# Shifts of integer score copies on one vector engine: two buffers an instruction, in place of a share on GpSimd

## Chip, cores and metric

One core of a Trainium2 chip. The metric is device time in microseconds (us). The kernel before has a median of 401.99 us over 4 runs (400.75 to 402.68). A measurement of this kernel can tell a difference of about 0.3% from none.

## What is computed

Two independent attention layers over 2048 tokens of width 448 with 16 heads of 28; the outputs are put side by side.

```python
def A(x, wq, wk, wv, wo):            # all heads share one k and one v
    q = (x @ wq) split in 16 heads;  k = x @ wk;  v = x @ wv
    p = softmax(q @ k.T * 28 ** -0.5)
    return concat_heads(p @ v) @ wo
def B(x, wqkv, wo):                  # each token sees itself and 7 tokens, 2 apart, before it
    q, k, v = split of x @ wqkv, 16 heads each
    return concat_heads(softmax over 8 positions (q . k) @ v) @ wo
out = concatenate([A(A_x, ...), B(B_x, ...)], axis=-1)
```

## The kernel before, in words

A is the bulk: 16 heads x 2048 queries x 2048 keys. Its scores are made in blocks of 128 keys by 512 queries, transposed, so that keys lie on partitions. There are 16 groups (4 stretches of 512 queries by 4 sets of 4 heads), and each has 64 blocks (16 key tiles by 4 heads): 1024 blocks. One matmul makes a block; up to four of them run beside each other on TensorE, one a strip of 32 rows (the QK step, `do_qk`, L1479). Each block then needs an exponential, and there are two ways:

- On ScalarE, an Exp from PSUM over two or three blocks at once (`act_choose`, L1227). Its five PSUM banks form two rings, of 3 and of 2 banks, which take turns. The result is in P.
- On VectorE, the code's D jobs (`dread`). A drain (L1526, name `dr`) turns the scores of a block, from one PSUM bank, into 16-bit integers that, read as bf16, are a coarse power of two. The result is the first of four variants in a buffer Z. Two more instructions, SBUF to SBUF, make the other variants: the first shift (L1534, `s1`) adds 32 to variant 0 and gives variant 1 (512 elements a partition); the second (L1541, `s2`) adds 64 to variants 0 and 1 and gives 2 and 3 (1024 elements). There are NZ = 6 such buffers. The four variants are multiplied by four differently weighted copies of v (WJ), which averages the coarseness out.

The PV step (`do_pv`, L1589) multiplies P or Z blocks by v, again up to four beside each other, and gathers a group in one PSUM bank. A closed group goes through `chain`: VectorE copies the bank to a buffer PVs (L988), SP sends the row of denominators to `den` by a DMA, VectorE takes reciprocals (L1004), SP sends them to DRAM and back, spread over partitions, to `bc`, and GpSimd or VectorE multiplies (L1034, `mul`). `outproj` (L662) multiplies by wo, VectorE or ScalarE moves the result to an output buffer (L1090, L1088), and SP or ScalarE issues the DMA to the output. B has 16 score blocks (L1320), each with an Exp on ScalarE (L1343) and a minimum with a mask (L1340), and its own PV step (L1287). Projections of both layers (L662) are "fills": work for TensorE between the QK steps.

The order on every engine is settled when the program is built. A planner in the kernel keeps a clock for each engine and lets the engine that is furthest behind pick its next step (`pe_choose`, `act_choose`, `spec_choose`), from costs and due times that are constants at the top of the file. `SCHED` resets some of these constants at given planned times. A few matter here. A drain's shifts wait in one list for VectorE or GpSimd; GpSimd takes a first shift only when VectorE's backlog is at least `GPB` = 1500 planned ns, and the second shift of a buffer stays on the engine that made the first. `put` with `port=True` keeps such VectorE and GpSimd steps from overlapping in the plan. A fill that is overdue may run over the planned start of the next QK step by up to `FTOL` ns. `DWAIT` says how long a QK step may be held for a bank for a D job. `dummy` (L1672, L1674) puts matmuls on zeros or weights whose result isn't used where TensorE's planned activity of the last 3.4 us is under `HAMLOW`. Each engine runs its list in order; a step waits on semaphores for what it reads and overwrites.

At the start (`plan_start`), the first 512 rows of x come in by two DMAs, from SP and from ScalarE's queue, each for all 128 partitions and two of the four rows that a partition holds. TensorE transposes them (L682); the other rows come by transposing DMAs on SP. GpSimd's queue makes constants, issues the DMAs of wB (B's weights, 1.2 MB), and then fills wB's unused part, woA, woB and `one` by memsets.

Of the kernel before, what the change touches and what calls it, by code (L numbers as in the profile page):

```python
# [6 lines left out]
ALU = mybir.AluOpType  # L7
AX = mybir.AxisListType
BF16 = mybir.dt.bfloat16
# [4 lines left out]
D = 448  # L14
# [31 lines left out]
def bk0(b, half):  # L46
# [3 lines left out]
    if b == 0 and half == 0:  # L50
# [6 lines left out]
AHEAD = 2  # L57
BT0 = 87
BDT = 38
DRATE = 0.3  # L60
# [3 lines left out]
TOL = 40.0  # L64
DWAIT = 100.0
FTOL = 250.0
FSAFE = 300.0
# [4 lines left out]
GP_S2 = 1010.0  # L72
GPB = 1500.0
GP_TT16 = 1010.0
# [8 lines left out]
HAMW = 3413.0  # L83
HAMLOW = 0.5
HAMTILE = 0.55
LATE = 1000.0
RINGD = 0.25
RINGB = 1200.0
PRESS = 2
PV3 = 8  # L90
JOBO = 0.0
JOBL = 1.0
XL0 = 4300.0
FILLN = 120.0
FILL0 = 8.0
FRATE = 0.036
FQUIET = 70

SCHED = ((0, {'HAMLOW': 0.5, 'HAMTILE': 0.55, 'FILLN': 120.0, 'FILL0': 8.0, 'PV3': 8, 'RINGB': 1200.0, 'PRESS': 2, 'DWAIT': 100.0, 'FTOL': 250.0, 'TOL': 40.0, 'JOBO': 0.0, 'LATE': 1000.0, 'FSAFE': 300.0}),
         (300, {'HAMLOW': 0.6, 'FTOL': 400.0, 'TOL': 20.0}),  # L100
         (330, {'FTOL': 250.0, 'TOL': 40.0, 'LATE': -5.0}),
         (355, {'HAMLOW': 0.5, 'FILL0': 4.0, 'RINGB': 1800.0, 'PRESS': 1, 'DWAIT': 300.0, 'LATE': 1000.0}),
         (375, {'HAMLOW': 0.8, 'FILL0': 8.0, 'RINGB': 1200.0, 'PRESS': 2, 'DWAIT': 200.0}))
VB0 = 27.0
WO0 = 70
# [48 lines left out]
class Spec:  # L154


    def __init__(self, engs, reads, writes, make, prio, dur, gate, name, hold, port):
        self.engs = engs
        self.reads = reads
        self.writes = writes  # L160
        self.make = make
        self.prio = prio
        self.dur = dur
        self.gate = gate
        self.name = name
        self.hold = hold
        self.port = port


# [33 lines left out]
class _Gen:  # L203
# [233 lines left out]
    def alloc(self, es):  # L437
# [28 lines left out]
        self.mask = sb([128, 2, 512], BF16, "mask")  # L466
        self.NPV = 4
        self.PVs = sb([128, self.NPV, 512], FP32, "PVs")
# [9 lines left out]
        self.oTnB = sb([128, 4, 4, 512], BF16, "oTnB")  # L478
        self.NO = 3
        self.ob = sb([128, self.NO, D], BF16, "ob")  # L480
        self.nr = sb([128, 2, 512], BF16, "nr")
# [19 lines left out]
    def plan_start(self):  # L501
        g = self
# [22 lines left out]

        def xA(q, b0, b1, lands):
            self.dma_op(q, g.xn[:, b0:b1, :], g.A_x[0, 0:512, :].rearrange("(p b) c -> p b c", b=4)[:, b0:b1, :],
                        writes=[res("xn")] if b0 == 0 else (), appends=[res("xn")] if b0 else (), lands=lands, name="x")
        xA("sp", 0, 2, XL0)
        xA("act", 2, 4, XL0)  # L530
        wA("act", g.wq, g.A_wq, D, "wq", 4500.0)
# [3 lines left out]
        for c in range(1, 4):  # L535
            for kt in range(4):
                self.dma_op("sp", g.xT_A[:, kt, 512 * c:512 * c + 512], g.A_x[0, 512 * c:512 * c + 512, x0(kt):x0(kt) + 128], writes=[res("xA", c, kt)],
                            transpose=True, issue=1310.0, lands=3000.0, moves=1200.0, name="xAt")
        dve(lambda e: e.memset(g.zero, 0.0), 100, writes=[res("zero")])
# [30 lines left out]
        for k in range(4):  # L570
# [6 lines left out]
                                     base=DH - 1, pattern=[[32, 4]], channel_multiplier=-1), 200, reads=[res("f2")], writes=[res("sel4")])  # L577
        self.dma_op("gp", g.wB[:, 0:3, :], g.B_wqkv[0:384, :].rearrange("(k p) c -> p k c", p=128), writes=[res("wB", 0)], issue=700.0, lands=9000.0, name="w")
        self.dma_op("gp", g.wB[64:128, 3, :], g.B_wqkv[384:448, :], writes=[res("wB", 1)], issue=700.0, lands=9000.0, name="w")
        gp(lambda e: e.memset(g.wB[0:64, 3, :], 0.0), 900, writes=[res("wB0")])  # L580
        gp(lambda e: e.memset(g.woA[:, :, :], 0.0), 1600, writes=[res("woA0")])
        gp(lambda e: e.memset(g.woB[:, :, :], 0.0), 1600, writes=[res("woB0")])
        gp(lambda e: e.memset(g.one[:, :], 1.0), 450, writes=[res("one")])
        gp(lambda e: e.memset(g.vst[:, :, :, DH:32], 0.0), 300, writes=[res("vB0")])
        gp(lambda e: e.memset(g.vst[:, :, :, DH:DH + 1], 1.0), 150, reads=[res("vB0")], writes=[res("vB1")])
# [41 lines left out]
    def load_xb(self, exp):  # L627
# [9 lines left out]
        def mk(eng, ns):  # L637
            return dict(dma=True, transpose=True, out=g.xT_B[:, kt, 512 * c:512 * c + 512], in_=src, reads=[tick],
                        writes=[self.res("xB", c, kt)], lands=3500.0, moves=1300.0)
        self.later(("sp",), (1310,), [tick], mk, prio=3, name="xBt")  # L640

# [455 lines left out]
    def plan(self):  # L1097
# [15 lines left out]
        self.ots = Slots(self.NOT)  # L1113
        self.outs = Slots(self.NO)
        self.obuf = [self.ob[:, k, :] for k in range(self.NO)]
        self.dens = Slots(self.NDEN)
# [9 lines left out]
        self.rowdummy = {}  # L1126
        self.nfill = 0
        for k in range(XFREE, self.NP):
            self.pslots.free.remove(k)
        self.bP = {}  # L1130
        self.pv0 = 0
        self.plan_start()
        self.make_fills()
        self.loop()
# [53 lines left out]
    def backlog(self, T):  # L1188

        return max(0.0, self.T["dve"] - T) + sum(s.dur["dve"] for s in self.pend if "dve" in s.engs and not s.hold  # L1190
                                                 and self.ready("dve", s.reads, s.writes) <= T + 200.0)

    def do_spec(self, s, eng):
        self.pend.remove(s)
        ns = s.dur[eng]
# [237 lines left out]
    def do_qk(self, jobs, kind, reads):  # L1433
# [33 lines left out]
        alljobs = list(jobs)  # L1467
        banks = list(ring)
        if dj is not None:
            self.take_job(dj)  # L1470
            alljobs.append(dj)
            banks.append(ok[0])
            self.banks[ok[0]].busy = True
        for b in ring:
            self.banks[b].busy = True
# [14 lines left out]
        self.nA += len(jobs)  # L1490
        if dj is not None:
            self.nD += 1
            self.dread(dj, self.banks[banks[-1]])

# [13 lines left out]
    def dread(self, job, bank):  # L1508
# [11 lines left out]
        def mk(eng, ns):  # L1520
            bank.busy = False

            def cb(o):
                unit(0, zr[0])
                self.later(("dve", "gp"), (200, GP_S1), [zr[0]], sh1, prio=1.2, name="s1", writes=[zr[1]], port=True)
            return dict(emit=lambda e: e.tensor_scalar(out=g.Z[:, z, 0, :], in0=g.bank(bank.i), scalar1=ZBIAS, scalar2=0.0, op0=ALU.add, op1=ALU.max),  # L1526
                        reads=[bank.res], writes=[zr[0]], took=ns + 95, cb=cb)
        self.later(("dve",), (600,), [bank.res], mk, prio=0.2, name="dr", writes=[zr[0]])

        def sh1(eng, ns):  # L1530
            def cb(o):
                unit(1, zr[1])
                self.later((eng,), (332 if eng == "dve" else GP_S2,), [zr[0], zr[1]], sh2, prio=1.1, name="s2", writes=[zr[2]], port=True)
            return dict(emit=lambda e: e.tensor_scalar(out=g.Z[:, z, 1, :], in0=g.Z[:, z, 0, :], scalar1=1.0, scalar2=32.0, op0=ALU.mult, op1=ALU.add),  # L1534
                        reads=[zr[0]], writes=[zr[1]], took=ns + 60, cb=cb)
# [165 lines left out]
    def pe_choose(self):  # L1701
# [23 lines left out]
        if f is not None:  # L1725
            ns = (f.list[f.i][2] if self.cur is not None else f.first[2])
            urgent = f.due * 1000 < T
            if room >= ns - (FTOL if urgent else TOL):
                self.do_fill(f)
                return  # L1730
# [51 lines left out]
```

## Time and profile before

| | |
|---|---|
| median of 4 runs | 401.99 us |
| the profiled execution's own time | 401.64 us |
| its span, first to last instruction | 399.7 us |
| TensorE busy | 385.6 us, 7178 matmuls |
| ScalarE busy | 381.5 us, 374 instructions |
| VectorE busy | 350.6 us, 787 instructions |
| GpSimd busy | 157.1 us, 197 instructions |
| granted TensorE clock | full in every stretch |

In the views, PE is TensorE's matmul side, PEld its weight load, ACT is ScalarE, DVE is VectorE, POOL is GpSimd, SP is the engine that issues most DMAs; a `q` after the name is that engine's sequencer. A group row names the line, the engine, the operation, out<-in, shapes, then xcount, busy us, mean ns of one, and after a second bar the idle time just before its instructions with what ended it. An instruction's listed duration reaches past the start of its successor on the same engine, since they are pipelined: what an instruction costs its engine is the step from its start to the next start. A timeline row starts with the start and the duration in us; a number in brackets at its end is the idle time before it.

### The profile page before, as it was taken

The numbers are of one execution on the slowest core, as the hardware profiler recorded it, in microseconds if no ns is written. First come the engines' busy times: TensorE is split into PE (matmuls) and PEld (weight loads), VectorE is DVE, ScalarE is ACT, GpSimd is POOL, SyncE is SP. The second block draws the span as 40 slices with busy tenths as digits, with TensorE's granted clock in tenths as the row PEclk, the third lists the DMA queues.
The fourth block names the chain that finished last, engine by engine and source line by source line (L and its number), as shares of the span: only waits on it lengthen the run. The fifth ranks groups of instructions, "written<-read, shape, count | busy, mean of one in ns | idle before, by whom it ended". The sixth has DMA issues, their size and how long they took to land.

```text
span 399.7 us, 16464 instructions
## 1 busy us (share of the span) xinstructions
PE 385.6 (96%) x7178; PEld 135.4 (34%) x7178; DVE 350.6 (88%) x787; ACT 381.5 (95%) x374; POOL 157.1 (39%) x197
## 2 busy tenths in 40 slices
PE   8999899999999999999999999999999999999995
PEld 4323232223233343333433223233332343433232
DVE  2787899989999889988989988989999999899973
ACT  3799999999999999999999999999999999999991
POOL 8700031461324343262375673343643516133440
PEclk9999999999999999999999999999999999999999
DMA  8956686143100112211101120010032202233121
GB/s 221 146 95 122 134 160 141 32 94 74 45 3 5 31 34 59 55 55 29 31 6 40 49 67 23 3 28 5 8 77 54 79 18 58 54 101 101 39 72 60
DMA packets 42531, 25.09 MB, mean 63 GB/s; under 512 B 28348, under 2 KB 37996, under 8 KB 42460
## 3 DMA queue, kind: packets, MB, share of 16 engines
q1 hardware_dynamic: 40332, 21.05, 23.6%
q0 software_dynamic: 736, 2.11, 2.0%
q8 instruction: 57, 0.93, 1.0%
q10 hardware_dynamic: 1392, 0.89, 0.7%
q14 instruction: 14, 0.11, 0.1%
HBM read 13.80 MB, written 6.02 MB: 50 GB/s over the span
## 4 chain that ended last, share of the span: by engine, by line
ACT 71%; PE 17%; DVE 9%; issue 1%; DMA 0%; DVEq 0%
ACT P L1227 69%; PE ps L662 5%; PE ps L1589 5%; PE ps L1479 5%; DVE Z L1526 3%; DVE Z L1541 2%; ACT P L1343 2%; DVE Z L1534 1%; PE ps L607 1%; DVE kT_B L884 1%; DVE sq L1090 1%; DMA den<-PVs 0%; DVE ob L1090 0%; PE ps L682 0%; PE ps L1672 0%
## 5 line engine op out<-in xcount | busy, mean ns | idle before, releaser
L1227 ACT ACTIVATE P<-ps 128x1536 bf16<-128x1536 f32 (+1 forms) x350 | 372.7, 1260 | 3.4 <-PE ps L1479 3.3
L1526 DVE TENSOR_SCALAR Z<-ps 128x512 int16<-128x512 f32 x213 | 144.3, 683 | 19.2 <-PE ps L1479 17.9
L1589 PE MATMUL ps<-P,vA 128*32 128x512 bf16 x811 | 145.9, 386 | 1.2 <-ACT P L1227 0.9
L1589 PE MATMUL ps<-Z,vA 128*32 128x512 bf16 x852 | 145.4, 385 | 1.5 <-DVE Z L1526 0.9
L1479 PE MATMUL ps<-qT_A,kT_A 29*128 29x512 bf16 x1024 | 136.8, 384 | 4.3 <-DVE Z L1526 1.1
L1534 POOL TENSOR_SCALAR Z<-Z 128x512 int16<-128x512 int16 x58 | 36.0, 622 | 142.3 <-DVE Z L1541 63.4
L1479 PEld LDWEIGHTS ps<-qT_A,kT_A 29*128 29x128 bf16 x1024 | 35.3, 90 | 119.8 <-ACT P L1227 53.2
L1541 DVE TENSOR_SCALAR Z<-Z 128x1024 int16<-128x1024 int16 x155 | 72.0, 471 | 0.8
L1541 POOL TENSOR_SCALAR Z<-Z 128x1024 int16<-128x1024 int16 x58 | 60.6, 1046 | 12.1 <-DVE Z L1541 6.0
L1589 PEld LDWEIGHTS ps<-Z,vA 128*32 128x32 bf16 x852 | 36.8, 94 | 36.8 <-issue 22.8
L1589 PEld LDWEIGHTS ps<-P,vA 128*32 128x32 bf16 x811 | 36.7, 94 | 36.3 <-issue 19.7
L1534 DVE TENSOR_SCALAR Z<-Z 128x512 int16<-128x512 int16 x155 | 48.5, 330 | 0.4
L662 PE MATMUL ps<-xT_B,wB 128*32 128x512 bf16 x512 | 39.3, 382 | 0.2
L1034 POOL TENSOR_TENSOR oTnB<-PVs,bc 128x512 bf16<-128x512 f32 x16 | 20.4, 1272 | 31.5 <-DVE Z L1541 18.2
L1034 POOL TENSOR_TENSOR oTn<-PVs,bc 128x512 bf16<-128x512 f32 x15 | 19.8, 1318 | 30.2 <-DVE Z L1534 9.2
L988 DVE COPY PVs<-ps 128x512 f32<-128x512 f32 x31 | 21.1, 682 | 0.6 <-PE ps L1287 0.3
L662 PE MATMUL ps<-xT_A,wq 128*32 128x512 bf16 x256 | 20.5, 383 | 0.4 <-DVE PVs L988 0.4
L662 PE MATMUL ps<-woA,oTn 128*32 128x448 bf16 x256 | 18.4, 355 | 0.2 <-issue 0.2
L662 PE MATMUL ps<-woB,oTnB 128*32 128x448 bf16 x256 | 18.2, 355 | 0.0
L662 PE MATMUL ps<-wB,xT_B 128*32 128x448 bf16 x256 | 17.8, 355 | 0.0
L662 PEld LDWEIGHTS ps<-xT_B,wB 128*32 128x32 bf16 x512 | 10.8, 95 | 13.3 <-issue 6.3
L1287 PE MATMUL ps<-P,vB 32*32 32x25 bf16 (+1 forms) x1344 | 15.1, 171 | 0.0
(97 smaller groups left out, 242.1 us busy)
## 6 DMA issues: line engine op xcount, KB each, us to landing
bc<-rec_scratch SPq DMA_DIRECT2D x124, 64.0 KB, 2.1
v_scratch<-kT_B SPq DMA_DIRECT2D x16, 128.0 KB, 2.1
out_dram<-sq SPq DMA_DIRECT2D x17, 112.0 KB, 2.1
out_dram<-ob SPq DMA_DIRECT2D x13, 112.0 KB, 1.9
vB<-v_scratch SPq DMA_DIRECT2D x2, 640.0 KB, 6.0
vB<-v_scratch SPq DMA_DIRECT2D x2, 608.0 KB
wB<-in_B_wqkv_dram POOLq DMA_DIRECT2D x1, 1008.0 KB, 7.5
den<-PVs SPq DMA_DIRECT2D x31, 8.0 KB
```

Source lines behind the costliest of these rows:

```text
L607: self.pe_op("full", lambda e: e.matmul(g.bank(4), g.zero[:, 0:128], g.zero[:, :], start=True, stop=True), 430, reads=[res("zero")], write ...
L662: ins = e.matmul(self.bank(bank, 32 * j, 32 * j + m, 0, n), lhs(j), rhs(j), start=start, stop=stop, tile_position=(0, 32 * j))
L988: return dict(emit=lambda e: e.tensor_copy(out=g.PVs[:, p, :], in_=g.bank(bank.i)), reads=[bank.res], writes=[self.pvs.res[p]], took=ns + ...
L1034: return dict(emit=lambda e: e.tensor_tensor(out=dst(z), in0=g.PVs[:, p, :], in1=g.bc[:, b, :], op=ALU.mult), reads=[self.pvs.res[p], self ...
L1227: op = self.put("act", lambda e: e.activation(g.P[:, 1536 * k:1536 * k + 512 * n], g.ps[:, lo:lo + 512 * n], ACT.Exp, scale=ASCALE), ns, n ...
L1287: ins = e.matmul(g.bank(bank, 32 * j, 32 * j + 32, q0, n), g.vB[32 * c:32 * c + 32, b, 4 * gg + j, :], g.P[32 * c:32 * c + 32, x:x + n], s ...
L1343: return dict(emit=lambda e: e.activation(g.P[:, x:x + 512], g.bank(bank.i), ACT.Exp, scale=ASCALE), reads=[bank.res], writes=[self.pslotr ...
L1479: ins = e.matmul(g.bank(b), g.kT_A[32 * j:32 * j + DH + 1, 128 * tb:128 * tb + 128], g.qT_A[32 * j:32 * j + DH + 1, gr.sc % 2, gr.g, :], s ...
L1526: return dict(emit=lambda e: e.tensor_scalar(out=g.Z[:, z, 0, :], in0=g.bank(bank.i), scalar1=ZBIAS, scalar2=0.0, op0=ALU.add, op1=ALU.max ...
L1534: return dict(emit=lambda e: e.tensor_scalar(out=g.Z[:, z, 1, :], in0=g.Z[:, z, 0, :], scalar1=1.0, scalar2=32.0, op0=ALU.mult, op1=ALU.ad ...
L1541: return dict(emit=lambda e: e.tensor_scalar(out=g.Z[:, z, 2:4, :], in0=g.Z[:, z, 0:2, :], scalar1=1.0, scalar2=64.0, op0=ALU.mult, op1=AL ...
L1589: ins = e.matmul(g.bank(b, 32 * j, 32 * j + 32), l, r, start=st, stop=sp, tile_position=(0, 32 * j))
```

## The change

- `GPB` becomes 1e9: GpSimd takes no first shift, and so no second.
- `pair`: where VectorE is to make a shift and another buffer's shift of the same kind is ready too, one instruction makes both. It reads and writes the two buffers by a pattern of two levels (2 x 512 or 2 x 1024 elements).
- Five buffers PVs in place of four.
- The buffers `ob` go; outputs use the four pieces of xT_A that held the first 512 rows, free by then.
- The input comes in by partitions: 64 partitions, all four rows, in each DMA.
- The DMAs of wB stand behind four memsets in GpSimd's queue.
- Planner's constants: SCHED goes; others change, FTOL from 250 to 100 and DWAIT from 100 to 200 among them, and the planned cost of a transposing DMA. `TWOD` is off, `SPARE` and `FSTART` are 0, so what they govern changes nothing.

```diff
-BT0 = 87
-BDT = 38
+BT0 = 90
+BDT = 36
-DWAIT = 100.0
-FTOL = 250.0
+DWAIT = 200.0
+FTOL = 100.0
-GPB = 1500.0
+GPB = 1e9
-HAMLOW = 0.5
-HAMTILE = 0.55
+HAMLOW = 0.61
+HAMTILE = 0.54
-RINGD = 0.25
-RINGB = 1200.0
-PRESS = 2
+RINGD = 0.22
+RINGB = 900.0
+PRESS = 1
-FILLN = 120.0
-FILL0 = 8.0
+FILLN = 124.0
+FILL0 = 4.0
-SCHED = ((0, {...}), (300, {...}), (330, {...}), (355, {...}), (375, {...}))
-VB0 = 27.0
+PAIR = True
+SCHED = ()
+VB0 = 29.0
...
-        self.NPV = 4
+        self.NPV = 5
...
-        def xA(q, b0, b1, lands):
-            self.dma_op(q, g.xn[:, b0:b1, :], g.A_x[0, 0:512, :].rearrange("(p b) c -> p b c", b=4)[:, b0:b1, :],
+        def xA(q, r, lands):
+            self.dma_op(q, g.xn[64 * r:64 * r + 64, :, :], g.A_x[0, 256 * r:256 * r + 256, :].rearrange("(p b) c -> p b c", b=4),
...
-                            transpose=True, issue=1310.0, lands=3000.0, moves=1200.0, name="xAt")
+                            transpose=True, issue=1480.0, lands=3300.0, moves=1300.0, name="xAt")
...
-        self.dma_op("gp", g.wB[:, 0:3, :], ...)
-        self.dma_op("gp", g.wB[64:128, 3, :], ...)
         gp(lambda e: e.memset(g.wB[0:64, 3, :], 0.0), 900, writes=[res("wB0")])
         gp(lambda e: e.memset(g.woA[:, :, :], 0.0), 1600, writes=[res("woA0")])
         gp(lambda e: e.memset(g.woB[:, :, :], 0.0), 1600, writes=[res("woB0")])
         gp(lambda e: e.memset(g.one[:, :], 1.0), 450, writes=[res("one")])
+        self.dma_op("gp", g.wB[:, 0:3, :], ...)
+        self.dma_op("gp", g.wB[64:128, 3, :], ...)
...
+        self.outs = Slots(4)
+        self.outs.res = [self.res("xA", 0, k) for k in range(4)]
+        self.obuf = [self.xT_A[:, k, 0:D] for k in range(4)]
...
+    def pair(self, s, T):
+        for o in self.pend:
+            if o is not s and o.name == s.name and self.ready("dve", o.reads, o.writes) <= T + 15.0:
+                a, b = sorted((s, o), key=lambda x: x.z)
+                v0, v1, n, add = (0, 1, 1, 32.0) if s.name == "s1" else (0, 2, 2, 64.0)
+                sl = slice(a.z, b.z + 1, b.z - a.z)
+                self.pend.remove(s)
+                self.pend.remove(o)
+                ns = 332 if s.name == "s1" else 600
+                ma, mb = a.make("dve", ns), b.make("dve", ns)
+                op = self.put("dve", lambda e: e.tensor_scalar(out=self.Z[:, sl, v1:v1 + n, :], in0=self.Z[:, sl, v0:v0 + n, :], scalar1=1.0, scalar2=add,
+                                                               op0=ALU.mult, op1=ALU.add), ns, ns + 60, ma["reads"] + mb["reads"], ma["writes"] + mb["writes"], name=s.name, port=True)
+                ma["cb"](op)
+                mb["cb"](op)
+                self.npair += 1
+                return True
+        return False
...
     def do_spec(self, s, eng):
+        if PAIR and eng == "dve" and s.z is not None and self.pair(s, self.T[eng]):
+            return
```

## Prediction

> **What bounds the kernel now.** I began with the page: busy shares and the chain that ended last.
>
> ```profile
> PE 385.6 (96%) x7178; PEld 135.4 (34%) x7178; DVE 350.6 (88%) x787; ACT 381.5 (95%) x374; POOL 157.1 (39%) x197
> ...
> ACT 71%; PE 17%; DVE 9%; issue 1%; DMA 0%; DVEq 0%
> ```
>
> Three engines are nearly full, and the chain lies on ScalarE. So I split the span at ScalarE's first Exp (12.28) and the end of its last (390.27), and asked for that stretch; columns after the length are busy us (instructions) of PE, PEld, DVE, ACT, POOL, then clock.
>
> ```profile
> 12.28:390.27 377.99, 369.67 (x6989) 127.96 (x6988) 342.27 (x757) 376.67 (x366) 146.44 (x169) 1.00 0.26 58
> ```
>
> ScalarE works 376.67 of 377.99 us. The listed durations overlap, so I took the step from each Exp's start to the next. The steady steps are 1.330 us for three blocks, 0.904 for two, 0.477 for one of B. The groups by shape give the counts:
>
> ```profile
> L1227 ACT ACTIVATE P<-ps 128x1024 bf16<-128x1024 f32 x239 | 243.0, 1127 | 1.2 <-PE ps L1479 1.2
> L1227 ACT ACTIVATE P<-ps 128x1536 bf16<-128x1536 f32 x111 | 171.6, 1546 | 2.2 <-PE ps L1479 2.1
> L1343 ACT ACTIVATE P<-ps 128x512 bf16<-128x512 f32 x16 | 11.5, 721 | 0.0
> ```
>
> 111 x 1.330 + 239 x 0.904 + 16 x 0.477 = 371.3. From first to last start the trace has 376.85 us, where the 365 steady steps make 370.42: **6.43 us are lost**. That is nearly all that a better interleaving can give; the rest needs fewer ScalarE blocks, or a shorter head (12.28) or tail (399.75 - 390.27 = 9.48).
>
> Where the 6.43 go, each late Exp traced to its QK step: 2.26 in 13 places where TensorE's weight load ahead waited for "issue", nothing the trace shows; 1.78 in 20 where TensorE was still in a projection, B or dummy group (0.42 of it in projections that had waited for a drain); 1.21 in two where QK waited for a drain; 0.30 others; 0.88 in delays under 25 ns. Of the 1.21, 1.14 are this place (timelines of DVE, PE, ACT):
>
> ```profile
> 46.60 0.25 DVE L1004 RECIPROCAL rec<-den 128x16 f32<-128x16 f32 x1 [1.29 <-DMA den<-PVs]
> ...
> 47.78 0.39 PE L1479 MATMUL ps<-qT_A,kT_A 29*128 29x512 bf16 x3 [1.10 <-DVE Z L1526]
> ...
> 48.22 1.94 ACT L1227 ACTIVATE P<-ps 128x1024 bf16<-128x1024 f32 x2 [0.98 <-PE ps L1479]
> ```
>
> A reciprocal waits for a DMA; the drain queued behind it in VectorE's order is late, then QK, then the Exp. GpSimd has no part in it.
>
> **GpSimd's shifts go.** Rows of both engines:
>
> ```profile
> L1534 POOL TENSOR_SCALAR Z<-Z 128x512 int16<-128x512 int16 x58 | 36.0, 622 | 142.3 <-DVE Z L1541 63.4
> ...
> L1541 DVE TENSOR_SCALAR Z<-Z 128x1024 int16<-128x1024 int16 x155 | 72.0, 471 | 0.8
> L1541 POOL TENSOR_SCALAR Z<-Z 128x1024 int16<-128x1024 int16 x58 | 60.6, 1046 | 12.1 <-DVE Z L1541 6.0
> ...
> L1534 DVE TENSOR_SCALAR Z<-Z 128x512 int16<-128x512 int16 x155 | 48.5, 330 | 0.4
> ```
>
> VectorE's means hide two sorts. With GpSimd idle the medians are 282 and 416 ns, with a GpSimd shift running the means are 535 and 678. One such place, where GpSimd's second shift runs from 151.86 to 152.91:
>
> ```profile
> 151.86 1.05 POOL L1541 TENSOR_SCALAR Z<-Z 128x1024 int16<-128x1024 int16 x1
> ...
> 152.53 0.65 DVE L1541 TENSOR_SCALAR Z<-Z 128x1024 int16<-128x1024 int16 x1
> ```
>
> Over all VectorE instructions the excess beside GpSimd's shifts is 13.5 us, beside its multiplies (which stay) 4.3. The Trainium skill's "SBUF — State Buffer" (Who interferes with whom) has VectorE and GpSimd take turns on a shared port pair, the loser blocked for the whole instruction. By the rule alone, GpSimd's 96.6 us of shifts could block VectorE for as much; by the rows it is 13.5, because the plan keeps them apart. I take 13.5.
>
> **VectorE makes them, partly in pairs.** The order after has 215 drains (213), 123 single first and 115 single second shifts, 46 paired first and 50 paired second. Single steps are 0.200 and 0.333 us. No row has two levels. From below: 512 more elements add 0.133, so 1024 in a pair take 0.333, and 2048 take 0.333 + 2 x 0.133 = 0.600. From above: half the rate past the fixed part (0.067) gives 0.600 and 1.133, or 46 x 0.267 + 50 x 0.533 = 38.9 us more. The nearest rows, contiguous 1024, stand with the first; taken. Shifts then cost 123 x 0.200 + 115 x 0.333 + 46 x 0.333 + 50 x 0.600 = 108.2 us, against 155 x 0.533 + 13.5 = 96.1. With 2 x 0.6 for the drains VectorE's stretch grows by 13.3, from 342.3 to 355.6 of some 376: from 91% to about 94%. Free time shrinks from 36 to 21 us. On the path this is nothing while drains come in time; the rival below prices it if not.
>
> **ScalarE.** 809 blocks of A in 349 Exps, against 811 in 350: one two-block step less, **-0.90**.
>
> **TensorE.** PV groups go from 470 to 467, QK steps from 350 to 349, at a step of 0.22 us: 0.9 us less work. It counts only where an Exp waits for a busy TensorE; 4.04 of the 6.43 lost (2.26 + 1.78) stand there, in 33 of 350 QK steps, so it is worth between 0 and -0.9. I take a third, **-0.30**. Twelve more dummies of about 0.2 us stand where the plan leaves a hole; priced at 0 (up to +0.5 should holes close on the chip).
>
> **Planner's constants.** FTOL from 250 to 100 ns lets overdue fills run over QK by 0.4 as much: (1.78 - 0.42) x 0.6 = **-0.82** (between 0 and -1.36). The stall at 46 us hangs on one DMA's landing beside transposing loads, for which the new plan allows more time; I take 0.7 of 1.14, **-0.80** (0 to -1.14). Less waiting on the port: of the 0.42 at fills held by drains I take two thirds, **-0.28** (0 to -0.42). The 2.26 of "issue" stays: TensorE has as many instructions. Losses: 6.43 - 0.30 - 0.82 - 0.80 - 0.28 = 4.23.
>
> **Head.** The input's rule speaks against the change. Its packets ran from 1.81 to 3.90 us (459 KB, 219 GB/s) and landed by 4.38; the transposes start at 5.38, behind warm-up matmuls, so 1.0 us is free. The skill's same page (Door 1; Can I just issue two DMAs to hit both halves?) gives 64 partitions half the ports, about 218 GB/s, and has two such halves serialize. By the row at its own rate nothing changes; by the rule, if the row was port-bound at all, 459 KB at 218 GB/s is the same 2.1 us; doubled to 4.2 it would be +1.1 us. Taken: 0, range 0 to +1.1. wB's DMAs move behind 1.24 + 1.61 + 1.61 + 0.19 us of memsets, to about 8.9; at 7.5 us to landing they are in by 16.4, first read at 28.6: 0, with 12 us of cover. The memsets come 1.5 us earlier; nobody waits. PVs copies (L988) idled 0.6 us in all, so the fifth buffer is worth 0 to -0.6; taken 0. Output buffers: casts to `ob` waited for PE, not for a buffer; 0.
>
> **Tail.** Before, VectorE's last chain:
>
> ```profile
> 392.53 0.71 DVE L979 STREAM_TRANSPOSE oTn<-nr 128x512 bf16<-128x512 bf16 x1
> 393.72 0.62 DVE L1090 CAST ob<-ps 128x448 bf16<-128x448 f32 x1 [0.48 <-PE ps L662]
> 394.26 0.61 DVE L1090 CAST sq<-ps 128x448 bf16<-128x448 f32 x1
> ```
>
> Two casts follow the last transpose; the last DMA is issued at 394.90, 1.65 after the transpose ended (393.25). In the order after, TensorE has 28 more matmuls of B's projection (7 groups of 0.19 us) behind A's last 16, and VectorE four casts. TensorE ends them 0.04 + 11 x 0.19 + 0.18 = 2.3 after the transpose, the last cast runs to 3.0, and so does its DMA's issue: **+1.35**.
>
> **Sum.** -0.90 - 0.30 - 0.82 - 0.80 - 0.28 + 1.35 = -1.75. Against the profiled execution (span 399.75, time 401.64): 401.64 - 1.75 = 399.89. Its time lies 0.35 under the median of the runs, so 400.2 is my forecast for the median.
>
> **Rivals.** (1) *The interleaving nearly closes* (14%): the losses fall to some 2.3 and the head gives nothing back: -0.90 - 4.1 + 1.35 = -3.65, 398.3; with the "issue" stalls (2.26) halved as well, 397.2. For it: TensorE has less work. Against: three engines stay over 90%. (2) *Nothing visible* (19%): new stalls or the input's +1.1 eat the 1.75; 400.8 to 403.2. The change does what it says, but GpSimd's shifts were off the path: drains held QK in two places only. (3) *VectorE's queue becomes the wait* (18%, slower): a pair holds the engine 0.133 or 0.267 us longer than a single shift, 46 x 0.133 + 50 x 0.267 = 19.5 us in all, and drains queue behind. Place: QK waiting for L1526. Before, weight loads of QK waited 22.2 us for drains and 1.21 reached ScalarE. Should a fifth of the 19.5 get through (+3.9) on top of the tail, without the planner's gains: -0.9 + 1.35 + 3.9 = +4.35, 406.3; at a tenth, +2.4, 404.4. To be slower by 0.3% (1.2 us) it needs 1.2 - 0.45 = 0.75 us of new waits if my other gains on the losses (2.20) fail, and 2.95 if they come. At half rate for the pairs, 38.9 us exceed the free 21 by 17.9, and the time is about 420 (402.0 + 0.45 + 17.9); a twentieth at most, within this case.
>
> **Numbers.** My forecast's case, -0.3% to -1%, has 49%: 398 to 400.8. Faster by over 0.3% (what a measurement can tell): 49 + 14 = 63%; within 0.3%: 19%; slower: 18%. The range runs from 397.0, just under the lower end of (1), to 404.4, the nearer end of (3), which leaves out some 9% above and 4% below.
>
> **What would show it.** Right: no GpSimd shift row; single shifts at 280 and 415 ns throughout; pairs stepping 0.33 and 0.60; 349 + 16 Exps; losses between starts near 4.2; a tail near 10.8; x landed before the transposes. Wrong: pairs over 0.85 us, QK waiting for L1526 over 30 us, several stalls over 0.5 us on ScalarE, or a first Exp later than 12.6.

## The result, and the profile after

The kernel after has a median of 399.48 us over 36 runs (399.07 to 404.04), the kernel before, run beside it on the same chips, 401.67 us over 57 (400.25 to 405.14). The ratio is 0.9947, 95% interval 0.9934 to 0.9961: 0.53% faster, or 2.2 us. The forecast was 400.2 from 401.99, or 0.45%. The profiled execution has a span of 397.6 us, against 399.75. Runs of either kernel at a lower granted clock take longer; at 0.998 or more the kernel after has a median of 399.45 (27 runs) and the kernel before, in the groups of the experiments below, 401.32 to 402.04 (42 runs), so the difference isn't one of the clock.

First the page of the kernel after, the same two parts as before: busy time of each engine, and the chain that ended last.

```profile
PE 385.2 (97%) x7223; PEld 133.1 (33%) x7223; DVE 361.4 (91%) x812; ACT 380.9 (96%) x374; POOL 61.1 (15%) x81
...
ACT 79%; PE 18%; DVE 2%; issue 0%; DVEq 0%
```

GpSimd's 96 us of shifts are gone (157.1 to 61.1). VectorE has 10.8 us more, and yet its share of the chain fell from 9% to 2%. The chain is ScalarE's more than before, so the next view is the stretch from the first Exp's start (12.36) to the last one's end (387.82); columns as in the prediction (length, then busy of PE, PEld, DVE, ACT, POOL, then clock).

```profile
12.36:387.82 375.46, 369.06 (x7026) 125.74 (x7025) 351.86 (x780) 375.42 (x365) 50.36 (x53) 1.00 0.27 59
```

VectorE went from 342.27 to 351.86 in it; I had summed 355.6. The groups by shape of the kernel after give the Exps and the shifts:

```profile
L1250 ACT ACTIVATE P<-ps 128x1024 bf16<-128x1024 f32 x238 | 252.8, 1198 | 0.0
L1250 ACT ACTIVATE P<-ps 128x1536 bf16<-128x1536 f32 x111 | 179.6, 1618 | 2.1 <-PE ps L1512 2.1
...
L1576 DVE TENSOR_SCALAR Z<-Z 128x1024 int16<-128x1024 int16 x115 | 48.7, 426 | 0.8
...
L1569 DVE TENSOR_SCALAR Z<-Z 128x512 int16<-128x512 int16 x123 | 35.0, 294 | 0.7
...
L1206 DVE TENSOR_SCALAR Z<-Z 128x2048 int16<-128x2048 int16 x50 | 34.2, 684 | 0.3
...
L1206 DVE TENSOR_SCALAR Z<-Z 128x1024 int16<-128x1024 int16 x46 | 18.8, 413 | 0.0
```

Single shifts have means of 294 and 426 ns where they had 330 and 471: nothing of GpSimd's is beside them but its multiplies. The pairs (L1206) step at 0.335 and 0.599 us from start to start (medians), where 0.333 and 0.600 were taken. So the two-level pattern costs nothing over a contiguous one here (the contiguous 1024 of the second shift step at 0.335 too).

From first to last Exp start, with the same three steady steps as before, the two profiles divide like this (us):

| | before | after | difference | predicted |
|---|---|---|---|---|
| first Exp starts | 12.28 | 12.36 | +0.08 | 0 |
| steady steps | 370.41 | 369.51 | -0.90 | -0.90 |
| lost between the starts | 6.43 | 4.75 | -1.68 | -2.20 |
| last Exp's start to the end | 10.62 | 10.97 | +0.35 | +1.35 |
| span | 399.75 | 397.60 | -2.15 | -1.75 |

The total came out as predicted to 0.4 us. Two of its terms did not, and a third (the head) was right in this pair of profiles by luck; that took the experiments to see.

What was lost, traced as before to the QK step of each late Exp: TensorE in fills 2.66 (before 1.78), behind PV 0.93 (2.52, of it 2.26 "issue"), QK that waited 0.19 (1.25), under 25 ns 0.97 (0.88). The weight loads of QK now wait half as long for drains. The row of the kernel before, then that of the kernel after:

```profile
PEld ps L1479 <- DVE Z L1526: 22.2, 50, 1.6
PEld ps L1512 <- DVE Z L1560: 10.9, 25, 0.5
```

The columns are total, times and longest. And the reciprocal that waited 1.29 us for a DMA at 46 us no longer has a bracket at its end, so it waited for nothing (VectorE's timeline of the kernel after):

```profile
47.13 0.24 DVE L1003 RECIPROCAL rec<-den 128x16 f32<-128x16 f32 x1
```

The tail. VectorE's last rows in the kernel after, then SP's last DMA issues:

```profile
390.07 0.71 DVE L978 STREAM_TRANSPOSE oTn<-nr 128x512 bf16<-128x512 bf16 x1
391.26 0.62 DVE L1089 CAST sq<-ps 128x448 bf16<-128x448 f32 x1 [0.48 <-PE ps L661]
391.81 1.98 DVE L1089 CAST xT_A<-ps 128x448 bf16<-128x448 f32 x3
```

```profile
393.05 1.09 SPq L334 DMA_DIRECT2D out_dram<-xT_A  x2
```

The transpose ends at 390.78 and the last cast at 393.79: 3.0 us, as predicted, where it was 1.65. But what follows the last issue is shorter. SP's first final wait passes 1.7 us after it, where before, with five output DMAs issued within 0.94 us, it took 2.4 us; and from there to the end SP takes 2.11 us in place of 2.48. So only 0.35 of the 1.35 is left. That it is the spacing of the issues which shortens the landing is not tested.

### The profile page after: what moved, and what is told of

It reads as the page before. It is cut to its first block, busy times and chain, and to the rows that moved or that the text cites. A ratio compares the mean times of both kernels' runs of the same rounds, so it can differ in the third digit from the quotient of the medians.

```text
span 397.6 us, 16416 instructions
## 1 busy us (share of the span) xinstructions
PE 385.2 (97%) x7223; PEld 133.1 (33%) x7223; DVE 361.4 (91%) x812; ACT 380.9 (96%) x374; POOL 61.1 (15%) x81
## 3 DMA queue, kind: packets, MB, share of 16 engines
q0 software_dynamic: 736, 2.11, 1.9%
## 4 chain that ended last, share of the span: by engine, by line
ACT 79%; PE 18%; DVE 2%; issue 0%; DVEq 0%
ACT P L1250 77%; PE ps L661 5%; PE ps L1624 5%; PE ps L1512 5%; ACT P L1366 2%; PE ps L606 1%; PE ps L1343 1%; PE ps L1310 0%; PE ps L681 0%; DVE Z L1560 0%; DVE xT_A L1089 0%; DVE sq L1089 0%; PE ps L1709 0%; DVE Z L1206 0%; DVE qT_A L834 0%
## 5 line engine op out<-in xcount | busy, mean ns | idle before, releaser
L1560 DVE TENSOR_SCALAR Z<-ps 128x512 int16<-128x512 f32 x215 | 146.4, 683 | 8.4 <-PE ps L1512 7.1
L1624 PE MATMUL ps<-P,vA 128*32 128x512 bf16 x809 | 140.3, 385 | 0.0
L1624 PE MATMUL ps<-Z,vA 128*32 128x512 bf16 x860 | 139.2, 384 | 0.2
L1206 DVE TENSOR_SCALAR Z<-Z 128x1024 int16<-128x1024 int16 (+1 forms) x96 | 52.2, 554 | 0.3
L1576 DVE TENSOR_SCALAR Z<-Z 128x1024 int16<-128x1024 int16 x115 | 48.7, 426 | 0.8
L1624 PEld LDWEIGHTS ps<-P,vA 128*32 128x32 bf16 x809 | 34.5, 94 | 32.3 <-issue 22.2
L1624 PEld LDWEIGHTS ps<-Z,vA 128*32 128x32 bf16 x860 | 33.3, 94 | 29.9 <-issue 19.0
L1569 DVE TENSOR_SCALAR Z<-Z 128x512 int16<-128x512 int16 x123 | 35.0, 294 | 0.7
L661 PE MATMUL ps<-woB,oTnB 128*32 128x448 bf16 x256 | 17.0, 356 | 0.0
L1343 PE MATMUL ps<-qT_B,kT_B 29*32 29x25 bf16 (+1 forms) x1344 | 14.9, 172 | 0.2 <-issue 0.2
```

The costliest lines, as they stand in the source:

```text
L661: ins = e.matmul(self.bank(bank, 32 * j, 32 * j + m, 0, n), lhs(j), rhs(j), start=start, stop=stop, tile_position=(0, 32 * j))
L1206: op = self.put("dve", lambda e: e.tensor_scalar(out=self.Z[:, sl, v1:v1 + n, :], in0=self.Z[:, sl, v0:v0 + n, :], scalar1=1.0, scalar2=ad ...
L1343: ins = e.matmul(g.bank(bank, 32 * c, 32 * c + 32, q0, n), g.kT_B[32 * j:32 * j + DH + 1, s, k0:k0 + 32], g.qT_B[32 * j:32 * j + DH + 1, s ...
L1576: return dict(emit=lambda e: e.tensor_scalar(out=g.Z[:, z, 2:4, :], in0=g.Z[:, z, 0:2, :], scalar1=1.0, scalar2=64.0, op0=ALU.mult, op1=AL ...
L1624: ins = e.matmul(g.bank(b, 32 * j, 32 * j + 32), l, r, start=st, stop=sp, tile_position=(0, 32 * j))
```

## Experiments

The theory to be tested (A): ScalarE's Exps set the end and VectorE has slack for all shifts; the gain is one Exp fewer and a better interleaving. Two rivals: (B) the gain comes from VectorE's shifts being no longer held up beside GpSimd's; (C) VectorE's queue is what counts, and the pairs are what makes room. Two further questions came up on the way: what the head and the tail really cost, and how much is owed to the constants. Medians of the kernel before differ by up to 1.3 us between groups of runs (401.56 to 402.85), and the granted clock differs too (mean 0.995 and 0.994 in the groups of experiments 1 to 4 and 5 to 8, 0.998 in that of 9 to 12). So a ratio of 1 to 8 flatters the changed kernel; where it matters, medians and spans of profiles are compared with those of the kernel after.

### 1. The same order, every pair as two single shifts

```diff
-  e.tensor_scalar(out=Z[:, sl, v1:v1 + n, :], in0=Z[:, sl, v0:v0 + n, :], ...)
+  for z in (a.z, b.z):
+      e.tensor_scalar(out=Z[:, z, v1:v1 + n, :], in0=Z[:, z, v0:v0 + n, :], ...)
```

> The changed kernel in its own order; only that each of the 96 two-buffer shifts is issued as two single ones behind each other. By the steps of the profile before, VectorE then works 46 x (2 x 0.200 - 0.333) + 50 x (2 x 0.333 - 0.600) = 6.4 us longer. Theory A (ScalarE's row of Exps sets the end, VectorE has slack): the losses between Exps grow by less than 1.2 us, the ratio to the kernel before stays within 0.3% of the changed kernel's 0.9947. Theory C (VectorE's queue is what counts, and pairing is where the gain comes from): at least 3 us of the 6.4 come back, a ratio of 1.002 or more.

Measured: 400.31 us, ratio 0.995 (0.9922 to 0.9978); span 398.9. Between the Exps 6.10 were lost, 1.35 more than with pairs, for 96 x 0.067 = 6.4 us more of VectorE. The other three profiles with the order of the kernel after (experiments 3, 4 and 9) lost 5.03 to 5.46, so the cost is 0.6 to 1.4 us: between a tenth and a fifth of VectorE's extra time gets through, the shares that my third rival had assumed for a queue that becomes the wait. Theory A had allowed 1.2, so the losses don't settle it; the ratio falls where A had it, and far from C's 1.002. The cost is small because the sum is small: without pairs, the same order would still beat the kernel before.

### 2. The same order, GpSimd busy again beside VectorE

Five scratch operations of 512 elements, which nobody reads, behind each of GpSimd's multiplies; what is computed is unchanged.

```diff
+ if name == "gp" and o.name == "mul":
+     for c in range(5):
...
+         eng.tensor_scalar(out=self.scr[...], in0=self.ident[...], scalar1=1.0, scalar2=32.0, ...)
```

> The changed kernel in its own order; GpSimd in addition makes five shifts of 512 elements into a scratch buffer nobody reads, behind each of its 31 multiplies: 155 x 0.62 = 96 us, as much as GpSimd's shifts took in the kernel before (96.6 us). The output is the same. Theory B (the blocked VectorE shifts, 13.5 us of excess before, were what the change gained by): VectorE's [...]shifts show 500 to 700 ns beside GpSimd's work again, some 10 to 15 us of excess, and most of the 2.1 us gained goes: ratio 0.999 or more. Theory A (the gain is in the order and in one Exp fewer): the excess comes back on VectorE, the time hardly: ratio 0.994 to 0.998.

Measured: 418.39 us, ratio 1.0391 (1.0341 to 1.0441); 22.8 us lost between the Exps. The groups by shape of this kernel, and the chain of its page:

```profile
L416 POOL TENSOR_SCALAR scr<-ident 128x512 int16<-128x512 int16 x155 | 109.4, 706 | 10.2
L1586 DVE TENSOR_SCALAR Z<-Z 128x1024 int16<-128x1024 int16 x115 | 54.1, 473 | 0.8
L1579 DVE TENSOR_SCALAR Z<-Z 128x512 int16<-128x512 int16 x123 | 46.6, 388 | 0.7
```

```profile
DVE 42%; PE 37%; ACT 15%; DMA 2%; issue 2%; SPq 0%; DVEq 0%
```

The 512-element shift's mean went from 294 to 388 ns and VectorE's share of the chain from 2% to 42%. Here 109.4 us of GpSimd work cost VectorE 29 us, spread where the plan didn't foresee it, and VectorE's 21 us of free time were used up. So the number of theory A was missed, and the mechanism of B is real: VectorE has little left. In the kernel before, 96.6 us of GpSimd shifts cost VectorE 13.5. The plan kept them apart: there 47 of VectorE's 310 shifts ran beside one of GpSimd's, here 115 of 334 beside a scratch operation. A multiply can also queue behind scratch operations in this kernel, so not all of the 18 us is the port.

### 3. The input by columns again, all else as after

"By columns" is the input of the kernel before, each DMA with all 128 partitions and two of their four rows; "by rows" is that of the kernel after, 64 partitions and all four rows.

```diff
-  self.dma_op(q, g.xn[64 * r:64 * r + 64, :, :], g.A_x[0, 256 * r:256 * r + 256, :]...)
+  self.dma_op(q, g.xn[:, 2 * r:2 * r + 2, :], g.A_x[0, 0:512, :]...[:, 2 * r:2 * r + 2, :])
```

> The changed kernel in its own order, with the input loaded as before: each DMA for all 128 partitions and two of their four rows. In the traces the first input landed by 4.38 us before and by 5.21 us after, the transposes start at 5.38 and 5.29. Theory A: the transposes wait for warm-up matmuls anyway, so the first Exp stays within 0.1 us of 12.36 and the ratio within 0.2% of 0.9947. Rival: the halves by rows were the gain or a cost at the head; then the first Exp moves by 0.5 us or more.

Measured: 398.85 us, ratio 0.9897 (0.9866 to 0.9928); span 397.4, first Exp at 11.92 instead of 12.36. The new input costs 0.44 us in this pair, more than theory A's 0.1 and just under the rival's 0.5. (The ratio looks better than the times: the median is 0.63 us under that of the kernel after.) The halves ran one after the other in the kernel after, ScalarE's packets from 2.15 to 3.31 and SP's from 3.07 to 4.26 us, where both ran side by side between 1.81 and 3.90 before. The x tile itself still came in time in this profile (5.21, transposes at 5.38). Late was what stands behind it on SP's queue: wk landed at 7.22, here at 5.87. How that reaches the Exp is shown with experiment 9.

### 4. SP's final waits in the order of the last landings

SP ends the kernel by waiting for every DMA semaphore, in the order in which each was first used. The waits take about 0.06 us each, some 30 of them, and those that stand behind a semaphore which lands last are paid after it.

```diff
  for d in ends:
+     final.pop(d.dsem, None)
      final[d.dsem] = d.dval
```

> The changed kernel in its own order; only the list of semaphores on which SP waits at the very end is put in the order of each semaphore's last DMA, not its first. In the trace after, SP takes about 30 such waits at 0.06 us each behind the last landing, 395.49 to 397.19. Theory: those for DMAs long landed then pass while the last one is under way, and 1.3 to 1.7 us go from the end: ratio 0.990 to 0.992. Rival: something else than the waits (a drain, the instruction loads at the end) sets the last 2 us, and nothing changes.

Measured: 398.21 us, ratio 0.9886 (0.9854 to 0.9917). From the last Exp's start to the end 9.67 instead of 10.97: -1.30, at the lower edge of the forecast. The stretch between the Exps lost 5.46 here, 4.75 in the kernel after, 5.04 in experiment 3 and 5.03 in 9, all in the same order of work; so the losses of one profile are good to some 0.4 us, and the kernel after had the lowest of the four (5.07 on average).

### 5 to 8. Parts undone, with the work planned anew

Four kernels change what the planner may do, so every later step moves.

```diff
5, in the kernel before:  -GPB = 1500.0   +GPB = 1e9
6, in the kernel after:   -PAIR = True    +PAIR = False
7, in the kernel after:   -GPB = 1e9      +GPB = 1500.0
8, in the kernel after:   the constants and SCHED of the kernel before; GPB stays 1e9
```

> The kernel before with one part of the change alone: GpSimd takes no shifts (GPB 1e9), no pairs; planned anew. The new order has 206 drains (213 before) and 818 blocks in 351 Exps, whose steady steps make 116 x 1.330 + 235 x 0.904 + 16 x 0.477 = 374.4 us, 3.1 more than before. Theory A (the end is ScalarE's Exps plus what is lost between them): the port excess goes, but the time grows by about 3 us: ratio 1.004 to 1.010. Theory B (freeing VectorE of the port is the gain): faster, ratio 0.995 to 0.998.

> The changed kernel without pairs (every shift alone on VectorE), planned anew: 214 drains, 810 blocks in 344 Exps, steady steps 122 x 1.330 + 222 x 0.904 + 16 x 0.477 = 370.6 us, as with pairs (370.4). VectorE has 6.4 us more to do. Theory A: ratio within 0.3% of 0.9947, with losses of 4 to 6 us. Theory C (pairing carries the gain): losses over 7 us, ratio 0.999 or more.

> The changed kernel with GpSimd allowed to take shifts again (GPB 1500), pairs kept, planned anew: 34 shift pairs go to GpSimd, 221 drains, 803 blocks in 349 Exps, steady steps 105 x 1.330 + 244 x 0.904 + 16 x 0.477 = 367.9 us, 2.5 less than in the changed kernel. Theory A: that is faster, ratio 0.987 to 0.992, unless the losses grow by as much. Theory B: GpSimd's shifts block VectorE's, the losses between Exps grow by more than the 2.5 us, ratio 0.996 or more, with places where the weight load of QK waits for issue or a drain beside a GpSimd shift.

> The changed kernel with all planner's constants of before (SCHED too), except that GpSimd takes no shifts: pairs, fifth buffer, head and output buffers as changed; planned anew: 219 drains, 805 blocks in 349 Exps, 110 pairs, steady steps 368.7 us, 1.7 less than the changed kernel. My prediction put 1.6 us of the gain on the constants' better fit (FTOL, times of transposing DMAs). If so: losses some 6 us or more, ratio 0.994 to 0.999. Rival: the constants do nothing by themselves, the structure does it: losses as in the changed kernel (4.8), ratio 0.988 to 0.992.

Measured:

| | median, us | ratio | lost between Exps | last Exp's end to the end | steps of TensorE planned after the last Exp's start |
|---|---|---|---|---|---|
| before | 401.67 | 1 | 6.43 | 9.5 | 29 |
| after | 399.48 | 0.9947 (0.9934 to 0.9961) | 4.75 | 9.8 | 31 |
| 5 | 425.30 | 1.056 (1.052 to 1.0601) | 7.62 | 27.6 | 127 |
| 6 | 406.91 | 1.0106 (1.007 to 1.0143) | 6.11 | 16.5 | 67 |
| 7 | 403.79 | 1.002 (1.0 to 1.004) | 6.28 | 14.9 | 54 |
| 8 | 417.28 | 1.0357 (1.0322 to 1.0392) | 10.41 | 23.3 | 100 |

All four came out slower than theory A had forecast. In 6 and 7 the ratio is where a rival had it, but not for the rival's reason: the losses were to exceed 7 us in 6 and to grow by more than 2.5 in 7, and came to 6.11 and grew by 1.53. The large differences aren't where my theories looked. Without GpSimd's shifts and without pairs (5 against before) the Exps lose 1.2 us more, but 18 us come at the end: the projections of B (`outproj` on woB), which TensorE should do between the Exps, are left over (over a third of the matmuls there are dummies on wq). So these four say little of shifts. Experiment 7 is the best witness: with GpSimd making 34 buffers' shifts again, the last Exp starts at 386.04, 0.6 us earlier than in the kernel after, and the span is 4.0 us longer: the end has grown by 5.1. What its time says against GpSimd's shifts is the plan's end, not the shifts. That the shifts cost something as well isn't excluded: between the Exps it lost 0.8 to 1.5 us more than the four profiles in the order of the kernel after.

### 9 and 10. The two edits of 3 and 4 together; and that of 4 in the kernel before

> The kernel after with two edits: the first 512 rows of x by columns of the tile again, as in the kernel before, and SP's final waits in the order in which the last DMA of each semaphore was issued. Same order of work on all engines. If the two sums add: the waits alone moved the stretch from the last Exp's start to the end from 10.97 to 9.64 us (-1.33), the columns alone moved the first Exp from 12.36 to 11.92 (-0.44), so the span should be 397.6 - 1.8 = 395.8 and the ratio to the kernel before 0.985 to 0.989. Rival: the columns' -0.44 is not of the columns but of the moment at which TensorE's transposes double their rate (which differed between the profiles: 16 transposes took 1.05 to 1.91 us); then the first Exp lies anywhere between 11.6 and 12.3, and the ratio is 0.987 to 0.991, no better than the waits alone.

> The kernel before with only the order of SP's final waits changed. If the serial waits after the last landing are a cost that both kernels carry, the stretch from the last Exp's start to the end falls from 10.62 by 1.0 to 1.4 us, and the ratio is 0.996 to 0.998. Rival: the kernel before issues four output DMAs within 0.9 us at its end and its last landings come 2.4 us after the last issue, so the landings, not the waits, set its end; then the gain is under 0.4 us and the ratio 0.999 to 1.0.

Measured: 9 has a median of 397.37 us, ratio 0.9902 (0.9876 to 0.9929), span 395.7. It is the fastest of all, 2.1 us under the kernel after by the medians and 1.9 by the spans. 10 has 400.32 us, ratio 0.997 (0.9949 to 0.999). The end fell from 10.97 to 9.67 in 9 and from 10.62 to 8.92 in 10 (by 1.70, where 1.0 to 1.4 was expected), so the waits are a cost of both kernels, though not the same: the 0.4 us by which they cost less after is part of the shorter tail.

The head of 9 came earlier than either theory had it: first Exp at 11.47. Two timelines show why. Rows of TensorE, first in experiment 4 (input by rows of the tile, as in the kernel after), then in 9 (by columns):

```profile
5.38 1.29 PE L682 MATMUL ps<-ident,P 128*128 128x128 bf16 x16
7.34 0.61 PE L662 MATMUL ps<-xT_A,wk 128*32 128x512 bf16 x8 [0.66 <-DMA wk<-in_A_wk_dram]
```

```profile
5.38 1.08 PE L682 MATMUL ps<-ident,P 128*128 128x128 bf16 x16
6.39 0.65 PE L662 MATMUL ps<-xT_A,wk 128*32 128x512 bf16 x8
```

In 4 the k projection waits for wk; in 9 it follows the 16 transposes at once. Those took from 1.05 to 1.91 us in the 14 profiles, since they step at 107 ns until some moment and at 56 ns from then on. That moment was at 6.4 us in experiment 3, before 5.4 in experiment 1, and with the last transpose or later in the profiles of before and after. The granted clock in the rows says 1.00 throughout, so "full in every stretch" does not hold for the head: the trace's own record of the clock begins only at that moment (6.41 us in experiment 3, 5.41 in 9, 6.97 in the kernel after), and the rows cannot tell what stood ahead of it. It lay between 4.15 and 7.28 us in the 14 profiles. The Trainium skill's "TensorE: Matmul & The Clock Gate" (Part 1: The HAM clock gate) gives the same two steps, 107 and 56 ns, and says that the change depends on where in a free-running window of 3.41 us the first matmul lands. The traces agree: the moment wanders by 3.1 us though the first matmul always starts at 1.25, and the one stretch at half clock within experiment 11 lasts 3.41 us (131.24 to 134.65), here in a row of the same columns as above:

```profile
131.20:134.60 3.40, 3.40 (x25) 0.64 (x27) 2.63 (x7) 2.35 (x3) 0.00 (x0) 0.51 0.00 0
```

In all eight profiles by rows the k projection starts 0.09 us after wk lands. In the six by columns wk had landed 0.2 us or more before it, and the projection followed the transposes. The first Exp comes 5.04 to 5.08 us after the k projection's start in all 14. So the input by columns lets the head follow the clock: first Exps at 12.28, 12.27, 11.92, 11.54, 11.47 and 11.29 in six profiles, 11.80 on average. By rows it is tied to wk: 12.26 to 12.76 in eight, 12.46 on average. The rows cost about 0.66 us, and the pair before/after hid it because both had the late moment. The x tile was late too in some profiles by rows: it landed at 5.14 to 5.61 us, and in four of them (experiments 2, 6, 7 and 11) the transposes began after 5.38 for it. The runs' spread is no witness: half of those of the kernel before lie within 1.2 us and of the kernel after within 0.44, but in experiment 9, by columns, half lie within 0.34.

### 11 and 12. One neutral constant, and the constants alone

```diff
11, in the kernel after:   -VB0 = 29.0   +VB0 = 28.0
12, in the kernel before:  the constants of the kernel after, no SCHED; GPB stays 1500
```

> The kernel after with one constant, the planned time at which B's value work begins, moved from 29 to 28 us and the work planned anew. Neither theory of shifts has anything to say on it: VectorE makes them all, 36 and 42 in pairs, 141 and 129 alone. Theory that the plan's end decides: the Exps still come to 117 x 1.330 + 230 x 0.904 + 16 x 0.477 less the last = 369.8 steady, with 5 +- 1 lost, but 59 steps of TensorE are left behind the last Exp where the kernel after has 31. In the four plans made anew so far the end grew by 0.186 us a step left (54: 14.9, 67: 16.5, 100: 23.3, 127: 27.6; the kernel after 9.8 at 31), so the end is 15.0, the span 403 to 404.5 and the ratio 1.006 to 1.012. Rival, that constants hardly matter and the pairs carry the gain: 0.992 to 0.998.

> The kernel before (GpSimd's shifts, no pairs, four PVs, old input) with the constants of the kernel after, SCHED gone, the work planned anew. Theory that the constants are fitted to one plan: 121 x 1.330 + 228 x 0.904 + 17 x 0.477 less the last = 374.7 steady, 6 to 7 lost, 126 steps of TensorE left behind the last Exp and so an end of 27 us; span 420 to 422, ratio 1.05 to 1.056. Rival, that the constants by themselves bring the gain (the losses from 6.4 to 4.8, whatever makes the shifts): 0.993 to 1.0.

Measured: 11 has 406.08 us, ratio 1.0117 (1.0074 to 1.0159), at the upper edge of the forecast, span 405.6, and 14.85 us from the last Exp's end to the end, where 15.0 was expected. It lost 6.60 between the Exps (4 to 6 expected), with the 3.41 us at half clock among them. 12 has 430.05 us, ratio 1.0669 (1.0617 to 1.0722), slower than expected, in part by the clock: its one run at 0.998 took 426.44. Its end is 30.4 us (27 expected). The profiled execution of 12 had a mean granted clock of 0.972, so its losses between the Exps aren't read.

TensorE's last rows in 11:

```profile
390.79 2.47 PE L661 MATMUL ps<-woB,oTnB 128*32 128x448 bf16 x44
392.98 2.55 PE L661 MATMUL ps<-woA,oTn 128*32 128x448 bf16 x48
...
396.77 4.06 PE L661 MATMUL ps<-woB,oTnB 128*32 128x448 bf16 x80
```

The last Exp ended at 390.73; all this comes behind it. A microsecond in the planned start of one kind of work makes the kernel 6.6 us slower, three times what the change gains. The rival that the pairs carry the gain whatever the constants falls, and so does the one that the new constants do: in the old code they cost 6 to 7%. Code and constants are fitted to each other, and a part taken out alone shows the misfit rather than its own worth. Only the experiments that keep the order (1 to 4, 9, 10) measure parts.

## Why the prediction held, step by step

- **ScalarE, -0.90**: measured -0.90, from the counts of 238 + 111 + 16.
- **VectorE's shifts, 0 on the path**: right as far as the profiles show. The pairs' steps were 0.335 and 0.599; the nearest rows, contiguous 1024, had priced them, and the half rate fell away. VectorE's time in the stretch of the Exps grew by 9.6 instead of 13.3. Rival 3 didn't come, since QK's wait for drains fell from 22.2 to 10.9. Experiments 1 and 2 show how near it was: 6.4 us more on VectorE cost 0.6 to 1.4, 29 us more cost 18.
- **FTOL, -0.82**: this step failed. Losses in fills rose from 1.78 to 2.66. The case against it is plain: planned with FTOL 250 in place of 100, the kernel after has the same instructions in the same order on every engine. So in this plan it decides nothing.
- **The 2.26 of "issue" stays**: failed too, in the other direction; 0.24 is left behind PV. "TensorE has as many instructions" was no reason. In the kernel before, 3 of these 13 places, with 0.71 of the 2.26 us, had GpSimd at work in the 0.6 us ahead, fewer than the half that chance would give, so its shifts can't be the cause of the rest. What was stays open. In experiment 2 the label grew on the same order of work, from 13.3 to 24.8 us at QK's weight loads, so it isn't only TensorE's own doing.
- **The stall at 46 us, -0.80 of 1.14**: gone wholly. The loss between 40 and 60 us fell from 1.22 to 0.34.
- **Less waiting on the port, -0.28, and TensorE's work, -0.30**: not separable. All four terms on the losses sum to -2.20; -1.68 was measured, with 0.4 of spread between profiles. (Four profiles in the order of after lost 5.07 on average, the two in the order of before, the kernel before and experiment 10, 6.54: -1.47.)
- **Head, 0**: mis-sized. It is about +0.66 (experiments 3 and 9 and the 14 first Exps), within the range of 0 to +1.1. The cover was looked for in front of the transposes, where x just had it in this profile (0.17 us to spare), and not for the DMA queued behind x. Here the rule that the prediction weighed, the Trainium skill's "SBUF — State Buffer" (Can I just issue two DMAs to hit both halves?), was right that the halves serialize: the trace has them one after the other, each about 1.2 us long. The pair took 2.1 us, as the prediction's estimate from 218 GB/s had it and no longer than before (2.09); it began 0.34 us later and x landed 0.8 us later, and why is not shown.
- **Tail, +1.35**: mis-sized, +0.35. The cast chain came as summed (3.0 us). Left out was that what follows the last issue has a length of its own: 0.7 us less to SP's first final wait, 0.37 less in the waits behind it.
- **Rivals**: (1), at 398.3, was nearer to coming true than it seemed: experiment 9 is at 397.4, though by head and end, not by the interleaving. Its losses are 5.0.

So the forecast was right in its size and in its path: ScalarE's Exps set the end, one fewer is worth 0.90, and VectorE takes the shifts without becoming the wait. In the losses it was right by luck: the fills came 1.70 us worse than forecast, the places of "issue" 2.02 better. The tail's surplus likewise stands against the head's. Which of the edits brought the smaller losses stays open, since every kernel that undoes one of them was planned anew.

## What to carry to other kernels

Where an order is planned from constants, look first at what is left behind the last instruction of the bounding engine: here each step of TensorE left there cost about 0.19 us (31 left 9.8 us, 127 left 27.6), and in the kernels planned anew that outweighed the question of which engine makes a shift. To price one part of such a change, keep the order and edit only the instruction. Of a DMA that gets slower, check what is queued behind it, not only who reads it.

## What was not expected of the hardware

The serial final waits of SP cost 1.3 us in the kernel after and 1.7 in the kernel before, by their order alone. A start whose length follows the moment at which matmuls go from 107 to 56 ns spreads the first Exp by 1 us over six profiles (11.29 to 12.28), which a DMA that lands late can hide (12.26 to 12.76 over eight).
